# Transposing q, k and u of two batches by DMA inside SBUF instead of on TensorE

## The chip, the cores and the metric

The kernel runs on one core of one Trainium2 chip. The metric is device time in microseconds (us) of one execution. The core has five instruction streams, each of which runs its own list in order: TensorE (PE), VectorE (DVE), ScalarE (ACT), GpSimd (POOL) and SyncE (SP), which here only issues DMAs. Matrix products land in PSUM (eight banks of 2 KB per partition); everything else lives in SBUF (128 partitions).

## The reference

Two layers follow each other, for 4 batches of 768 positions. The first is a gated linear recurrence over 8 heads of width 48:

```python
for t in range(S):
    state = alpha[:, :, t, :, None] * state + np.einsum('bhd,bhe->bhde', k[:, :, t], v[:, :, t])
    y[:, :, t] = np.einsum('bhd,bhde->bhe', q[:, :, t], state)
```

Its output, with the heads side by side, is x of shape (4, 768, 384). The second layer mixes along the positions with a matrix of rank 32 and then applies a two-layer perceptron (384 to 1536 to 384):

```python
xt = x.transpose(0, 2, 1)
h = xt @ U @ V
u = x + h.transpose(0, 2, 1)
ch = np.maximum(u @ w_ch1, 0.0) @ w_ch2
return u + ch
```

## The kernel before

**Tiling.** Each batch is cut into 6 chunks of 128 positions, and the recurrence works on 2 chunks at a time: three stages per batch, `stage_gla`, twelve in all. Within a chunk the recurrence becomes matrix products. ScalarE takes the logarithm of alpha (L350, tile lt), TensorE sums it along the positions (L358, L360), and ScalarE makes exp of the sums and of their negatives (aa and ai, L368 and L369). k is multiplied by ai and q by aa (L374), which gives rk and rq, with positions on the partitions and every head padded from 48 to 64 columns. For the score product (L406) both must stand with the head dimension on the partitions. So TensorE transposes each 128x128 block of rk and of rq (L383, 8 blocks for k and 8 for q in a stage) into a PSUM bank, and ScalarE (L289) or VectorE (L291) copies the bank to SBUF as kt and qt. VectorE masks the scores (L416, tile pm), TensorE makes the update of the state (L441, L448), which VectorE scales (L451, tile st), and y from state and scores (L468, L474), which ScalarE writes to xb (L486).

**Mixing.** `stage_mix` makes the rank-32 product (L499, L506, tile utx). The first batch has a path of its own. For the other three, TensorE multiplies utx with V for each chunk (L524), VectorE adds that to xb (L525), which gives u, and TensorE transposes u in three groups of 6 blocks (L534), which ScalarE copies to uT (L542).

**Perceptron.** `mlp1` makes 24 groups of 3 products per batch (L553), each 384 columns wide, with the relu on ScalarE (L563) or VectorE (L565). `mlp2` makes 6 output chunks of 12 products (L574), adds u on VectorE (L583, tile ou) and stores (L584).

**Order.** A planner at build time (`Plan.run`) sets the order of all of it. Each operation is added with its engine, a cost in nanoseconds, what it reads and writes, and a priority (lower goes first). The planner simulates the engines with these costs and writes each engine's operations out in the order in which it started them. On the chip each engine then keeps that list strictly, whatever the real durations are. An engine whose next instruction waits does nothing else. Buffers are rotating pools, so a tile may also wait until the earlier user of its slot is done.

**Transfers.** All DMAs go through SP's one list: for each batch alpha, k, q and v, 1.18 MB each in runs of 192 bytes (48 float32 values), the six parts of the two weight matrices (768 KB each, cast to bfloat16 on GpSimd, L291), the two small matrices U and V, and 24 stores of 192 KB. A store waits in that list for VectorE's sum, and whatever stands behind it waits too.

**Fill.** Up to the first batch's mixing, the planner puts products without use (L587) into TensorE's gaps.

Of the kernel before, what the change touches and what calls it, by code (L numbers as in the profile page):

```python
# [49 lines left out]
class Op:  # L50
    __slots__ = ("eng", "cost", "fn", "prio", "deps", "bufs", "n", "end", "users", "est", "i")


class Plan:
# [11 lines left out]
    def add(self, eng, cost, fn, r=(), w=(), prio=0.0, after=(), kind=None):  # L66
# [24 lines left out]
        op.bufs = []  # L91
        for k in list(r) + list(w):
            b = k[0] if isinstance(k, tuple) else k
            if isinstance(b, Buf) and b not in op.bufs:
                op.bufs.append(b)
        for b in op.bufs:
            b.left += 1
        self.ops.append(op)
        return op

    def run(self):
# [8 lines left out]
        clock = {}  # L110
# [4 lines left out]
        while todo:  # L115
# [42 lines left out]
            if eng == "SP":  # L158
                clock[eng] = max(t + 450.0, dma)
# [29 lines left out]
def kernel(  # L189
# [50 lines left out]
    u_in = const.tile([128, NC, R], FP32, name="u_in")  # L240
    vm_in = const.tile([128, S], FP32, name="vm_in")
# [16 lines left out]
    pms = Pool(slots("pm", 4, [C, 2, HP, C], BF16))  # L258
# [3 lines left out]
    uts = Pool(slots("uT", 2, [128, NCT, S], BF16))  # L262
# [17 lines left out]
    mlps = [every, every, every, every]  # L280
# [12 lines left out]
    def load_low_rank():  # L293
        P.add("SP", 500, lambda: nc.sync.dma_start(u_in, moe_U.rearrange("(c p) r -> p c r", p=128)), w=["u_in"], prio=0.3)
        for g in range(4):
            P.add("SP", 400, lambda g=g: nc.sync.dma_start(vm_in[32 * g : 32 * g + R, :], moe_V), w=[("vm_in", g)], prio=0.3)
        P.add("POOL", 350, lambda: nc.gpsimd.tensor_copy(u_sb, u_in), r=["u_in"], w=["u"], prio=300)
        P.add("POOL", 820, lambda: nc.gpsimd.tensor_copy(vm_sb, vm_in), r=[("vm_in", g) for g in range(4)], w=["vm"], prio=300)

    def load_big():  # L300
# [6 lines left out]
        for i, (src, dst) in enumerate(parts):  # L307
# [7 lines left out]
            P.add("SP", 2000, lambda src=src, stage=stage: nc.sync.dma_start(stage(), src), w=[(t, i)], prio=0.5 if i < 3 else 0.6)  # L315
# [14 lines left out]
    def stage_gla(b, g, sprev, xb, ins):  # L330
# [59 lines left out]
        for src, dst, eng, cost in ((rk, kT, "ACT", 1015), (rq, qT, eqt, 1015 if eqt == "ACT" else 640)):  # L390
            tb = Buf(gen)
# [100 lines left out]
    def stage_mix(b, xb, uT):  # L492
# [14 lines left out]
        if b == 0:  # L507
            P.fill_end = op
            for hf in range(2):
                for j in range(NCT):  # L510
# [9 lines left out]
                    P.add(eng, 550 if eng == "DVE" else 490, lambda hf=hf, j=j, tb=tb, eng=eng: copy(eng, uT()[:, j, hf * TW : (hf + 1) * TW], tb()[:, 0, 0:TW]), r=[tb], w=[(uT, hf, j)], prio=pr)  # L520
            return utx
        for c in range(NC):
            hb = Buf(mlp)
            P.add("PE", mm(DM), lambda c=c, hb=hb: nc.tensor.matmul(hb()[:, 0, 0:DM], lhsT=vm_sb[:, c * C : (c + 1) * C], rhs=utx(), start=True, stop=True), r=[utx, "vm"], w=[hb], prio=pr + 1)  # L524
            P.add("DVE", 550, lambda c=c, hb=hb: nc.vector.tensor_tensor(xb()[:, c, :], xb()[:, c, :], hb()[:, 0, 0:DM], op=ALU.add), r=[hb, (xb, c)], w=[(xb, c)], prio=pr)  # L525
            if c % 2 == 1:
# [12 lines left out]
                def f_ev(c=c, ub2=ub2):  # L539
                    t = bf(ub2())[:, 0 : 2 * NCT * C].rearrange("p (c2 j t) -> p c2 j t", c2=2, j=NCT)  # L540
                    dst = uT()[:, :, (c - 1) * C : (c + 1) * C].rearrange("p j (c2 t) -> p c2 j t", c2=2)
                    nc.scalar.copy(dst, t)  # L542
# [3 lines left out]
    def mlp1(b, uT, h1, tt):  # L546
        for jt in range(NJ):
            hb = Buf(mlps[b])
            pr = 5000 + b * 1000 + tt * 100 + jt * 8

            def f(jt=jt, hb=hb):
                for ct in range(NCT):
                    nc.tensor.matmul(  # L553
                        hb()[:, 0, 0:TW], lhsT=w1_sb[:, ct, jt * 128 : (jt + 1) * 128],
                        rhs=uT()[:, ct, tt * TW : (tt + 1) * TW], start=(ct == 0), stop=(ct == NCT - 1),
# [3 lines left out]
            if b == 0:  # L559
                need = [(uT, tt, j) for j in range(NCT)]  # L560
            P.add("PE", mm(TW, TW, TW), f, r=need + [("w1", jt // 4)], w=[hb], prio=pr)
# [5 lines left out]
    def mlp2(b, xb, h1, c, utx):  # L567
        hb = Buf(mlps[b])
        pr = 5000 + b * 1000 + 100 + (c % 3) * 33 + (0 if c < 3 else 100)
        for g in range(3):  # L570

            def f(g=g):
                for jt in range(4 * g, 4 * g + 4):
# [4 lines left out]
                if g == 2 and utx is not None:  # L578
                    nc.tensor.matmul(hb()[:, 0, 0:DM], lhsT=vm_sb[:, c * C : (c + 1) * C], rhs=utx(), start=False, stop=True)

            P.add("PE", mm(*[DM] * (5 if g == 2 and utx is not None else 4)), f, r=([utx] if utx is not None else []) + [(h1, jt) for jt in range(4 * g, 4 * g + 4)] + [("w2", g)], w=[hb], prio=pr + g)
# [51 lines left out]
```

## Time and profile before

| | |
|---|---|
| median of 3 runs | 181.5 us (180.69 to 182.88) |
| the profiled execution | 180.38 us |
| its span, first to last instruction | 178.7 us |
| TensorE busy in the span | 166.2 us (93%) |
| VectorE, ScalarE, GpSimd busy | 94.0, 86.5, 52.7 us |
| share of TensorE in the chain that ended last | 65% |
| share of waits for DMA in that chain | 17% |

The profiled execution took 1.7 us more than its span, and 1.1 us less than the median. A matmul's busy time (326 ns for 384 columns) is the time from its start to its modelled end. Matmuls overlap, so the time that one adds to a dense row of them is read from the chain, which merges such a row: 39 of L553 took 6.34 us, 163 ns each.

### The profile page before, as it was taken

What the parts mean: (1) busy time and instruction counts of PE and PEld (TensorE: products, weight loads), DVE (VectorE), ACT (ScalarE), POOL (GpSimd) and SP (SyncE); (2) the same over time, 40 slices, a digit from 0 to 9 for tenths busy, and PEclk for the clock granted to TensorE, in tenths of its full rate; (3) what the DMA queues carried; (4) which work ended last, traced back from release to release, by engine and by line L of the source; (5) the groups of instructions that cost most, each with busy time, mean ns of one, the idle gap of its engine ahead of it and who ended that gap; (6) DMA issues with size and microseconds to landing.
All of it is one profiled execution on the core that took longest, in us unless ns stands there. A gap on an engine that the chain in (4) does not pass through costs nothing.

```text
span 178.7 us, 4275 instructions
## 1 busy us (share of the span) xinstructions
PE 166.2 (93%) x1821; PEld 107.8 (60%) x1821; DVE 94.0 (53%) x159; ACT 86.5 (48%) x142; POOL 52.7 (29%) x52
## 2 busy tenths in 40 slices
PE   5997888999999996988999999999999999999992
PEld 4775665555666754655666566755566565656560
DVE  2022991643327775458676577667485432544421
ACT  2387684645891344894783847401555310422200
POOL 4000197760469600497416567000000000000000
PEclk9999999999999999699999999999999999999999
DMA  4987999996977868899889300111101112101212
GB/s 111 262 257 221 261 287 391 370 321 191 261 224 225 254 204 246 275 259 262 257 230 252 117 15 33 48 46 44 48 0 44 48 46 88 44 0 48 85 49 88
DMA packets 32068, 29.08 MB, mean 163 GB/s; under 512 B 1584, under 2 KB 30768, under 8 KB 32048
## 3 DMA queue, kind: packets, MB, share of 16 engines
q1 hardware_dynamic: 32048, 28.81, 53.5%
q8 instruction: 14, 0.23, 0.6%
q14 instruction: 6, 0.05, 0.1%
HBM read 24.08 MB, written 4.72 MB: 161 GB/s over the span
## 4 chain that ended last, share of the span: by engine, by line
PE 65%; DMA 17%; SPq 6%; DVE 5%; ACT 3%; issue 2%; POOL 1%; DVEq 0%; ACTq 0%; POOLq 0%
PE ps L553 24%; PE ps L574 22%; DMA io<-in_alpha_dram 7%; DMA io<-in_q_dram 6%; SPq L327 4%; DMA io<-in_v_dram 4%; PE ps L474 3%; PE ps L383 3%; DVE pm L416 3%; PE ps L406 3%; SPq L584 2%; PE ps L468 2%; PE ps L441 1%; PE ps L524 1%; ACT lt L350 1%
## 5 line engine op out<-in xcount | busy, mean ns | idle before, releaser
L553 PE MATMUL ps<-uT,w_sb 128*128 128x384 bf16 x288 | 52.9, 326 | 0.0
L574 PE MATMUL ps<-w_sb,h1t 128*128 128x384 bf16 x288 | 52.4, 326 | 0.0
L563 ACT ACTIVATE h1t<-ps 128x384 bf16<-128x384 f32 x48 | 23.7, 493 | 37.7 <-PE ps L553 37.4
L574 PEld LDWEIGHTS <-h1t 128*128 128x128 bf16 x288 | 27.2, 98 | 17.1 <-issue 0.3
L553 PEld LDWEIGHTS <-w_sb 128*128 128x128 bf16 x288 | 26.9, 98 | 16.2 <-issue 0.3
L565 DVE TENSOR_SCALAR h1t<-ps 128x384 bf16<-128x384 f32 x48 | 26.7, 557 | 16.6 <-PE ps L553 14.8
L416 DVE TENSOR_TENSOR pm<-ps,maskc 128x1024 bf16<-128x1024 f32 x22 | 26.8, 1221 | 5.5 <-PE ps L406 4.9
L583 DVE TENSOR_TENSOR ou<-xb,ps 128x384 f32<-128x384 bf16 x24 | 13.3, 553 | 29.2 <-PE ps L574 20.5
L374 POOL TENSOR_TENSOR rk<-io,ai 128x768 bf16<-128x768 f32 x9 | 14.8, 1643 | 25.7 <-ACT ai L368 18.9
L289 ACT COPY kt<-ps 128x1024 bf16<-128x1024 bf16 x12 | 12.1, 1015 | 13.1 <-PE ps L383 6.1
L291 POOL CAST rv<-io 128x768 bf16<-128x768 f32 x12 | 9.6, 829 | 23.6 <-DMA io<-in_v_dram 23.6
L486 ACT CAST xb<-ps 128x768 bf16<-128x768 f32 x12 | 9.6, 798 | 13.8 <-PE ps L474 13.7
L374 POOL TENSOR_TENSOR rq<-io,aa 128x768 bf16<-128x768 f32 x9 | 14.8, 1645 | 4.1 <-DMA io<-in_q_dram 2.1
L587 PE MATMUL ps<-fill_in,ident 128*128 128x256 bf16 x87 | 13.6, 316 | 1.9 <-POOL ident masks.py:199 1.9
L350 ACT ACTIVATE lt<-io 128x768 bf16<-128x768 f32 x12 | 9.6, 841 | 9.7 <-DMA io<-in_alpha_dram 9.7
L525 DVE TENSOR_TENSOR xb<-xb,ps 128x384 bf16<-128x384 bf16 x18 | 9.5, 550 | 6.0 <-PE ps L524 5.9
L587 PEld LDWEIGHTS <-ident 128*128 128x128 bf16 x87 | 9.4, 113 | 4.1 <-POOL ident masks.py:199 1.9
L368 ACT ACTIVATE ai<-ps 128x768 bf16<-128x768 f32 x12 | 9.9, 822 | 0.3 <-PE ps L360 0.3
L369 ACT ACTIVATE aa<-ps 128x768 bf16<-128x768 f32 x12 | 10.0, 830 | 0.0
L291 POOL CAST w_sb<-io 128x1536 bf16<-128x1536 f32 x6 | 8.8, 1469 | 3.9 <-DMA io<-in_moe_w_ch_dram 3.9
L474 PE MATMUL ps<-rv,pm 128*128 128x48 bf16 x192 | 8.9, 184 | 1.1 <-DVE pm L416 1.1
L406 PE MATMUL ps<-qt,kt 48*128 48x128 bf16 x192 | 9.0, 218 | 0.5 <-ACT xb L486 0.5
(57 smaller groups left out, 157.4 us busy)
## 6 DMA issues: line engine op xcount, KB each, us to landing
io<-in_moe_w_ch_dram SPq DMA_DIRECT2D x6, 768.0 KB, 9.7
out_dram<-ou SPq DMA_DIRECT2D x24, 192.0 KB, 1.9
vm_in<-in_moe_V_dram SPq DMA_DIRECT2D x4, 96.0 KB, 2.6
u_in<-in_moe_U_dram SPq DMA_DIRECT2D x1, 96.0 KB, 6.1
io<-in_alpha_dram SPq DMA_DIRECT2D x4, 0.2 KB, 11.3
io<-in_k_dram SPq DMA_DIRECT2D x4, 0.2 KB, 10.2
io<-in_q_dram SPq DMA_DIRECT2D x4, 0.2 KB, 10.5
io<-in_v_dram SPq DMA_DIRECT2D x4, 0.2 KB, 8.9
```

The source lines that it names most:

```text
L289: nc.scalar.copy(dst, src)
L291: ENG[eng].tensor_copy(dst, src)
L374: ENG[eng].tensor_tensor(dst()[:, :, :, 0:D], ch(src), fac().rearrange("t g (h d) -> t g h d", d=D), op=ALU.mult)
L406: nc.tensor.matmul(s2[:, par, p, :], lhsT=kT()[o : o + D, i, p, :], rhs=qT()[o : o + D, i, p, :], start=(p == 0), stop=(p == HP - 1),)
L416: nc.vector.tensor_tensor(pmi().rearrange("t two hp c -> t (two hp) c"), sc().rearrange("p two (hp c) -> p (two hp) c", c=C), maskc.to_bro ...
L474: nc.tensor.matmul(y2[:, par, p, :], lhsT=pm[i]()[:, par, p, :], rhs=rv()[:, i, 2 * p + par, :], start=(i == 0 and p == 0 and last is None ...
L553: nc.tensor.matmul(hb()[:, 0, 0:TW], lhsT=w1_sb[:, ct, jt * 128 : (jt + 1) * 128], rhs=uT()[:, ct, tt * TW : (tt + 1) * TW], start=(ct == ...
L563: P.add("ACT", 500, lambda jt=jt, hb=hb: nc.scalar.activation(h1()[:, jt, :], hb()[:, 0, 0:TW], AF.Relu), r=[hb], w=[(h1, jt)], prio=100)
L565: P.add("DVE", 560, lambda jt=jt, hb=hb: nc.vector.tensor_scalar_max(h1()[:, jt, :], hb()[:, 0, 0:TW], 0.0), r=[hb], w=[(h1, jt)], prio=100)
L574: nc.tensor.matmul(hb()[:, 0, 0:DM], lhsT=h1()[:, jt, (c % 3) * C : (c % 3 + 1) * C], rhs=w2_sb[:, jt, :], start=(jt == 0), stop=(jt == NJ ...
L583: P.add("DVE", 550, lambda: nc.vector.tensor_tensor(ou(), xb()[:, c, :], hb()[:, 0, 0:DM], op=ALU.add), r=[hb, (xb, c)], w=[ou], prio=100)
L587: P.fill_fn = lambda i: nc.tensor.matmul(ps[:, i, 0:256], lhsT=ident, rhs=fill_in, start=True, stop=True)
```

## The change

For the third and fourth batch (b = 2 and 3; batches are counted from 0 in the code and below) three kinds of transpose leave TensorE, and one DMA instruction on SP does each instead, from SBUF to SBUF. In each of these batches' six stages there is one for rk to kt and one for rq to qt, 128 partitions by 1024 elements (256 KB, 8 blocks). In the mixing there are two per batch, from xb to uT, 128 by 1152 elements (288 KB, 9 blocks). With the 132 TensorE transposes their copies out of PSUM go too: 6 of L289 and 6 of L542 on ScalarE and 6 of L291 on VectorE. There are 16 transposing DMAs in all.

The same edit changes some other things. In batch 1 q is scaled on VectorE instead of GpSimd, and its transposed copy is made on ScalarE instead of VectorE. The pool of masked scores has 6 slots instead of 4. uT is laid out by chunk instead of by block of columns. U and V are staged in a slot of the load pool. The three loads of the second weight matrix get a later priority. In batch 0's mlp1 the second half comes sooner, and mlp2's last product of batch 0 (L579 before) is an operation of its own.

```diff
-        op.i = len(self.ops)
+        op.i, op.hold = len(self.ops), hold
...
             if eng == "SP":
-                clock[eng] = max(t + 450.0, dma)
+                clock[eng] = max(t + op.hold, dma)
...
-    u_in = const.tile([128, NC, R], FP32, name="u_in")
-    vm_in = const.tile([128, S], FP32, name="vm_in")
...
-    pms = Pool(slots("pm", 4, [C, 2, HP, C], BF16))
+    pms = Pool(slots("pm", 6, [C, 2, HP, C], BF16))
...
-    uts = Pool(slots("uT", 2, [128, NCT, S], BF16))
+    uts = Pool(slots("uT", 2, [128, NC, NCT, C], BF16))
...
     def load_low_rank():
-        P.add("SP", 500, lambda: nc.sync.dma_start(u_in, moe_U.rearrange("(c p) r -> p c r", p=128)), w=["u_in"], prio=0.3)
+        t = Buf(io)
+
+        def u_in():
+            return t()[:, 0 : NC // 2, :].rearrange("p a (two r) -> p (a two) r", r=R)
+
+        def vm_in():
+            return t()[:, 16:28, :].rearrange("p a w -> p (a w)")
+
+        P.add("SP", 500, lambda: nc.sync.dma_start(u_in(), moe_U.rearrange("(c p) r -> p c r", p=128)), w=[(t, 4)], prio=0.3)
...
-            P.add("SP", 2000, lambda src=src, stage=stage: nc.sync.dma_start(stage(), src), w=[(t, i)], prio=0.5 if i < 3 else 0.6)
+            P.add("SP", 2000, lambda src=src, stage=stage: nc.sync.dma_start(stage(), src), w=[(t, i)], prio=0.5 if i < 3 else 1.15)
...
         ek = "DVE" if first else "POOL"
-        eq = "DVE" if first else "POOL"
+        eq = "DVE" if b in (0, 1) else "POOL"
         ev = "POOL"
-        eqt = "ACT" if first else "DVE"
-        split = (-1, 1, 1)[g] if first else -1
+        eqt = "ACT" if b in (0, 1) else "DVE"
+        split = (-1, 1, 1)[g] if b in (0,) else -1
...
         for src, dst, eng, cost in ((rk, kT, "ACT", 1015), (rq, qT, eqt, 1015 if eqt == "ACT" else 640)):
+            if b in (2, 3):
+                P.add("SP", 1000, lambda src=src, dst=dst: nc.sync.dma_start_transpose(dst().rearrange("p g e c -> p (g e) c"), src().rearrange("t g h w -> t (g h w)")), r=[src], w=[dst], prio=pr / 1000 - 1, hold=1250.0)
+                continue
             tb = Buf(gen)
...
             P.add("DVE", 550, lambda c=c, hb=hb: nc.vector.tensor_tensor(xb()[:, c, :], xb()[:, c, :], hb()[:, 0, 0:DM], op=ALU.add), r=[hb, (xb, c)], w=[(xb, c)], prio=pr)
+            if b in (2, 3):
+                if c % 3 == 2:
+                    P.add("SP", 1100, lambda c=c: nc.sync.dma_start_transpose(uT()[:, c - 2 : c + 1].rearrange("p c j t -> p (c j) t"), xb()[:, c - 2 : c + 1, :].rearrange("p c m -> p (c m)")), r=[(xb, c - i) for i in range(3)], w=[(uT, c // 3, j) for j in range(NCT)], prio=pr / 1000 - 1, hold=1300.0)
+                continue
             if c % 2 == 1:
...
-            pr = 5000 + b * 1000 + tt * 100 + jt * 8
+            pr = 5000 + b * 1000 + tt * (100 if b else 50) + jt * (8 if b else 4)
...
-                        rhs=uT()[:, ct, tt * TW : (tt + 1) * TW], start=(ct == 0), stop=(ct == NCT - 1),
+                        rhs=uT()[:, 3 * tt : 3 * tt + 3, ct, :], start=(ct == 0), stop=(ct == NCT - 1),
...
-            if b == 0:
+            if b == 0 or b in (2, 3):
                 need = [(uT, tt, j) for j in range(NCT)]
```

The planner writes a new order from this. The first place is SP's list around the loads of batches 2 and 3; line numbers are those of each kernel's own file. Before, from the last two stores of batch 0, the loads of v of batch 2 (io_88) and of alpha, k, q and v of batch 3 stand in a row:

```order
L584 DMA out_dram<-ou_150 128x384
L584 DMA out_dram<-ou_151 128x384
L327 DMA io_88<-in_v_dram 128x48x48
L327 DMA io_89<-in_alpha_dram 128x48x48
L327 DMA io_90<-in_k_dram 128x48x48
L327 DMA io_91<-in_q_dram 128x48x48
L327 DMA io_86<-in_v_dram 128x48x48
L584 DMA out_dram<-ou_149 128x384
```

In the changed program the same stretch, from the first transposing DMA on (L398 is the transpose, L333 a load, L596 a store):

```order
L398 DMA_TRANSPOSE kt_123<-rk_98 128x8x128
L333 DMA io_86<-in_v_dram 128x48x48
L398 DMA_TRANSPOSE qt_126<-rq_93 128x8x128
L398 DMA_TRANSPOSE kt_124<-rk_99 128x8x128
L398 DMA_TRANSPOSE qt_127<-rq_94 128x8x128
L398 DMA_TRANSPOSE kt_125<-rk_96 128x8x128
L398 DMA_TRANSPOSE qt_128<-rq_95 128x8x128
L333 DMA io_88<-in_alpha_dram 128x48x48
L333 DMA io_89<-in_k_dram 128x48x48
L596 DMA out_dram<-ou_149 128x384
L333 DMA io_84<-in_q_dram 128x48x48
L333 DMA io_85<-in_v_dram 128x48x48
```

The load of batch 2's v now stands behind the first transpose, and all four loads of batch 3 stand behind six transposes. Each of these waits for a product of GpSimd (rk or rq).

The second place is the list of GpSimd after the casts of the first weight matrix (tile w_sb from 128x3x512 is the first matrix, from 128x1536 the second; rk and rq are the products of batch 1). Before:

```order
L291 CAST w_sb<-io_90 128x3x512 x2
L291 CAST w_sb<-io_91 128x3x512
L291 CAST w_sb<-io_91 128x1536
L291 CAST w_sb<-io_86 128x1536 x2
L374 TENSOR_TENSOR rk_101<-io_88,ai_118 128x16x48
L374 TENSOR_TENSOR rk_98<-io_88,ai_119 128x16x48
L374 TENSOR_TENSOR rq_95<-io_89,aa_115 128x16x48
```

And in the changed program, with L289 the cast and L380 the product:

```order
L289 CAST w_sb<-io_89 128x3x512 x2
L289 CAST w_sb<-io_84 128x3x512
L380 TENSOR_TENSOR rk_99<-io_86,ai_116 128x16x48
L289 CAST w_sb<-io_84 128x1536
L380 TENSOR_TENSOR rk_96<-io_86,ai_117 128x16x48
L289 CAST w_sb<-io_87 128x1536 x2
L380 TENSOR_TENSOR rk_97<-io_86,ai_118 128x16x48
```

The casts of the second weight matrix now come between the products for k of batch 1, and the three products for q have left the list. On SP the loads of the second matrix stand, likewise, behind those of alpha and k of batch 1.

On TensorE the list is the same up to batch 0's mlp1. In batch 2, before, the scores of the first stage stood behind 6 products of that batch's predecessor's mlp1 (L553); now they stand behind 39 of them in a row. In batch 3 now the first scores also stand behind 39 (L564 in the new file), of batch 2's mlp1, and the 16 small products of the state's update.

More of the change, by code (lines that the diff above doesn't have):

```diff
@@ L50 @@
 class Op:
-    __slots__ = ("eng", "cost", "fn", "prio", "deps", "bufs", "n", "end", "users", "est", "i")
+    __slots__ = ("eng", "cost", "fn", "prio", "deps", "bufs", "n", "end", "users", "est", "i", "hold")
 class Plan:
@@ L279 @@
     mlp0 = banks((6,), (7,), (4,), (5,))
-    mlps = [every, every, every, every]
+    mlps = [banks(*[(i,) for i in s]) for s in (range(8),) * 4]
     def bf(bank):
@@ L569, in mlp2 @@
         pr = 5000 + b * 1000 + 100 + (c % 3) * 33 + (0 if c < 3 else 100)
[L570 removed]
+        for g in range(NJ // 4):
             def f(g=g):
[L573 removed]
+                for jt in range(4 * g, 4 * (g + 1)):
                     nc.tensor.matmul(
@@ L577, in f @@
                     )
-                if g == 2 and utx is not None:
-                    nc.tensor.matmul(hb()[:, 0, 0:DM], lhsT=vm_sb[:, c * C : (c + 1) * C], rhs=utx(), start=False, stop=True)
-            P.add("PE", mm(*[DM] * (5 if g == 2 and utx is not None else 4)), f, r=([utx] if utx is not None else []) + [(h1, jt) for jt in range(4 * g, 4 * g + 4)] + [("w2", g)], w=[hb], prio=pr + g)
+            P.add("PE", mm(*[DM] * 4), f, r=[(h1, jt) for jt in range(4 * g, 4 * (g + 1))] + [("w2", g * 4 // 4)], w=[hb], prio=pr + g)
+        if utx is not None:
+            P.add("PE", mm(DM), lambda: nc.tensor.matmul(hb()[:, 0, 0:DM], lhsT=vm_sb[:, c * C : (c + 1) * C], rhs=utx(), start=False, stop=True), r=[utx], w=[hb], prio=pr + 9)
         ou = Buf(outs)
```

21 lines of the change are left out of this document (10 added, 11 removed).

## The prediction

> **What bounds the kernel now.** I read the page first, for the shares and the slices, then a table by stretch, then the chain of waits.
>
> ```profile
> span 178.7 us, 4275 instructions
> ...
> PE 166.2 (93%) x1821; PEld 107.8 (60%) x1821; DVE 94.0 (53%) x159; ACT 86.5 (48%) x142; POOL 52.7 (29%) x52
> ...
> PE   5997888999999996988999999999999999999992
> ...
> PEclk9999999999999999699999999999999999999999
> DMA  4987999996977868899889300111101112101212
> ```
>
> TensorE is busy 93% of the span, without a hole in the second half. The DMA engines are the opposite: near full until the 22nd slice (98 us), then almost idle. So an average says little, and the stretches must be read apart (PE, PEld, DVE, ACT, POOL, granted clock, DMA share, GB/s):
>
> ```profile
> 47.00:65.00 18.00, 17.83 (x227) 11.84 (x226) 10.87 (x17) 8.07 (x14) 12.08 (x9) 1.00 0.80 234
> 65.00:82.00 17.00, 14.63 (x199) 9.78 (x198) 9.41 (x16) 13.66 (x22) 7.07 (x5) 0.90 0.87 249
> 82.00:100.00 18.00, 17.20 (x271) 11.25 (x271) 12.92 (x20) 10.63 (x18) 8.25 (x7) 1.00 0.91 260
> 100.00:175.00 75.00, 75.00 (x657) 45.94 (x654) 40.22 (x70) 26.39 (x48) 8.82 (x7) 1.00 0.12 43
> ```
>
> From 100 to 175 us TensorE is busy all of the time, and from 82 to 100 it lacks 0.8 us. Only from 65 to 82 us is there a gap of 2.4 us, with a granted clock of 0.90. So what leaves TensorE in batches 2 and 3 should leave the time, unless TensorE's fixed list then waits for something. The chain of waits, in order of time, gives what each piece costs there:
>
> ```profile
> 32.59 6.40 PE ps L553 x39
> ...
> 74.64 6.65 DMA io<-in_v_dram
> ...
> 90.25 0.45 PE ps L383 x8
> ...
> 91.70 0.17 PE ps L358
> 91.94 0.18 PE ps L358
> 92.20 0.24 PE ps L441 x8
> 92.44 0.19 PE ps L448
> ...
> 95.99 0.20 PE ps L468 x8
> 96.19 0.31 PE ps L474 x8
> 96.50 0.33 PE ps L406 x8
> ...
> 100.82 0.43 PE ps L499 x6
> ...
> 109.03 0.34 PE ps L534 x6
> ...
> 151.72 6.34 PE ps L553 x39
> ```
>
> A product of 384 columns costs 6.34 / 39 = 0.163 us in the dense row, eight transposes of k or q 0.45 us, and six of u 0.34 us; a chunk's running sum with its four narrow products takes 0.25 (from 91.70 to 91.94 and on to 92.20). The time at 74.64 is the load of batch 2's v, the one place after 72 us where the chain runs through a DMA.
>
> **What leaves TensorE.** Per stage 8 transposes of rk and 8 of rq, in six stages: 12 groups of eight. In the mixing 3 groups of six per batch: 6 groups. So 12 x 0.45 + 6 x 0.34 = 5.4 + 2.0 = **7.4 us**. Of the twelve, four stand before 82 us, where TensorE is not full; if those gave nothing, 5.6 us would be left. ScalarE and VectorE lose their copies too:
>
> ```profile
> L289 ACT COPY kt<-ps 128x1024 bf16<-128x1024 bf16 x12 | 12.1, 1015 | 13.1 <-PE ps L383 6.1 <-DVE ou L583 4.1 <-issue 2.8
> ...
> L542 ACT COPY uT<-ps 128x768 bf16<-128x768 bf16 x9 | 7.2, 800 | 3.8 <-PE ps L534 3.8
> ...
> L291 DVE COPY qt<-ps 128x1024 bf16<-128x1024 bf16 x9 | 6.2, 684 | 2.5 <-PE ps L383 1.3 <-ACT uT L542 1.2
> ```
>
> That is 6 x 1.0 + 6 x 0.8 = 10.9 us of ScalarE and 6 x 0.68 = 4.1 us of VectorE, both half idle in these stretches; I count nothing for it. In batch 1 q's scaling moves between these two rows:
>
> ```profile
> L374 POOL TENSOR_TENSOR rq<-io,aa 128x768 bf16<-128x768 f32 x9 | 14.8, 1645 | 4.1 <-DMA io<-in_q_dram 2.1 <-PE ps L524 1.9
> ...
> L374 DVE TENSOR_TENSOR rq<-io,aa 128x768 bf16<-128x768 f32 x3 | 2.8, 955 | 3.3 <-DMA io<-in_q_dram 3.3
> ```
>
> GpSimd loses 3 x 1.65 us and VectorE gains 3 x (0.96 - 0.68) = 0.8 us, while ScalarE takes 3 x 1.0 us of copies. From 47 to 65 us VectorE is busy 10.9 of 18 us and ScalarE 8.1, so that hides; without the cover it would cost at most those 0.8 and 3 us. Six slots for pm and the other layouts move no bytes that anyone waits for: zero.
>
> **What one transposing DMA costs.** The trace has none. Call p the time for which one keeps SP's list or the DMA engines, whichever is longer. The nearest rows are the loads and the stores, on the same queue (start and held time of SP, then size and time to landing):
>
> ```profile
> 69.16 5.27 SPq L584 DMA_DIRECT2D out_dram<-ou  x2
> 74.64 0.70 SPq L327 DMA_DIRECT2D io<-in_v_dram  x1
> 75.80 4.12 SPq L327 DMA_DIRECT2D io<-in_alpha_dram  x1
> 80.38 4.20 SPq L327 DMA_DIRECT2D io<-in_k_dram  x1
> 85.04 4.36 SPq L327 DMA_DIRECT2D io<-in_q_dram  x1
> 89.86 4.18 SPq L327 DMA_DIRECT2D io<-in_v_dram  x1
> ...
> out_dram<-ou SPq DMA_DIRECT2D x24, 192.0 KB, 1.9
> ```
>
> Loads follow each other every 4.7 us (80.38 to 85.04). One is 6,144 runs of 192 bytes, 1.18 MB. A transpose moves 256 KB in 1,024 rows of 256 bytes: by runs 4.7 / 6 = 0.8 us, by bytes 1.0 us. If the crossing cuts it into pieces of 32 bytes, 8,192 runs, it is 6.3 us. So p lies between 0.8 and 6.3 us. I take 1.2, near the byte figure, since a run's length and its end in SBUF are close to the load's; the code's planner reckons 1.25, a number of the code that no row confirms. A store lands 1.9 us after its issue, of which 0.8 is its bytes: 1.1 us for landing.
>
> These rows are the ground for a fast transpose, and one rule speaks against it. The Trainium skill (VectorE: DVE Perf Modes, section on the three transpose paths) gives a DMA transpose of one 128x128 block 1,309 ns against 390 ns on TensorE, and advises TensorE where PSUM will do. If the eight blocks each paid that, p would be 10.5 us (an estimate from that page), and the sum would end near 265 us; no run here shows it. On its side the trace has TensorE's block at 0.45 / 8 = 0.06 us in a dense row, far below that page's 390 ns.
>
> **Where TensorE waits for the transposes.** Batch 2 begins where GpSimd makes its first product, and mlp1 of batch 1 fills TensorE:
>
> ```profile
> 38.80 1.47 POOL L291 CAST w_sb<-io 128x1536 bf16<-128x1536 f32 x1 [0.67 <-DMA io<-in_moe_w_ch_dram]
> ...
> 71.86 1.64 POOL L374 TENSOR_TENSOR rk<-io,ai 128x768 bf16<-128x768 f32 x1 [10.46 <-ACT ai L368]
> 75.43 1.64 POOL L374 TENSOR_TENSOR rq<-io,aa 128x768 bf16<-128x768 f32 x1 [1.94 <-PE ps L524]
> ...
> 78.23 0.65 PE L553 MATMUL ps<-uT,w_sb 128*128 128x384 bf16 x3
> ```
>
> rk is made at 73.5 us, so the first transpose issues at about 74.6, where v's load stood. v's load follows (4.7 us), then q's transpose, which lands at 74.6 + p + 4.7 + p + 1.1 = 80.4 + 2p: 82.8 us. TensorE starts mlp1 at 78.2 and has 39 products ahead of the scores, to 84.6. No wait up to p = 2.1. The next two pairs have 12 and 16 wide products and some groups of eight (0.2 to 0.33 us each) between them: 4.1 and 5.1 us against 2p.
>
> The tighter place is batch 3. Its loads stand behind six transposes: alpha issues at 79.3 + 6p = 86.5 us instead of 75.8 (GpSimd's last product, five of 1.65 us after 75.4, is ready at 83.7). v then issues at 100.6; before, it issued at 89.9 and GpSimd began its cast at 100.1, so now it lands at 110.8 and its cast ends at 111.6. TensorE's list first needs it for the state's update of batch 3. From 84.6 us stand ahead of that, in the changed list, 111 products of 384 columns (18.1 us), 22 groups of eight (6.0 us), four of L448, six running sums and L499 (2.7 us): 111.4 us. That is a wait of **0.2 us**, and 6 us more for each microsecond of p. For batch 3's own transposes the DMA engines are idle (share 0.12), and TensorE's 39 products with the 16 small ones give 6.9 us for the first pair; 3.9 and 4.7 us for the others. The transposes of u have 32 and more wide products (5.2 us) against 1.1p + 1.1: hidden.
>
> **The second weight matrix.** Its loads come behind alpha and k of batch 1, 8.4 to 9.4 us later. Its last part landed at 38.8 before, so now at 47.2 to 48.2, and is cast by 48.7 to 49.7. TensorE starts mlp1 of batch 0 at 32.6, has 72 products (11.7 us), two stages' sums and one group of transposes (1.5 us) and 1.7 us of other products ahead: 47.5. A wait of 1.2 to 2.2 us. The 2.4 us of gap between 65 and 82 us can take some of it, since batch 1 starts earlier: I count **1.0 us**.
>
> **Sum.** 180.4 - 7.4 + 0.2 + 1.0 = 174.2 us for a profiled execution; the median lies 1.1 above it, so **175.3 us**. What is late next is still TensorE's list, with the same end.
>
> **Rivals.**
>
> *Faster than that* (under 173): nothing is lost in front, and the gap from 65 to 82 us closes because k of batch 1 comes earlier: 180.4 - 7.4 - 2.4 = 170.6 to 173. Against it stands the second weight matrix. Chance 0.07.
>
> *It evens out.* p is about 1.95 to 2.4. Then TensorE waits 0.2 + 6 x (p - 1.2) for batch 3's v, 4.7 to 7.4 us, and the 7.4 are gone: 180 to 182.5 us. For it: nothing in the trace crosses partitions by DMA. Chance 0.09.
>
> *Slower.* p above 2.4; one mechanism, batch 3's loads queued behind six transposes on SP while TensorE's list waits. At p = 3, v costs 0.2 + 10.8 = 11.0, and batch 3's later pairs (6 us against 3.9 and 4.7) 3.4: 180.4 - 7.4 + 1.0 + 14.4 + 1.1 = 189.5 us. It decides from p = 2.2, where it equals the gain. A waiting TensorE may also run slower after it, as the 6 in the clock row, at 71 to 76 us, stands in the one stretch with gaps. Chance 0.11.
>
> *Block by block.* Eight landings in series, 8 x 1.1 + 1.0 = 9.8 us. Batch 3's v would come 52 us late, its six transposes take 59 us, and two of u and one mlp follow: about 260 us. The rows say that a 192 KB store pays its landing once, not per piece. This is the result that the skill's block price, above, would give. Chance 0.03.
>
> **How the numbers follow.** My forecast (p up to 1.95) has the remaining 0.70, from 173 to 180 us. About 1% (1.8 us) is what a measurement of this kernel can tell from no change. Faster by over 1%: 0.70 + 0.07 = 0.77. Within 1%: 0.09. Slower: 0.11 + 0.03 = 0.14. The range reaches down to 171 us, into the faster case, and up to 183.5, past the one that evens out; it leaves out the slower cases (0.14) and the lowest few hundredths.
>
> **What would show it.** TensorE's rows L383 and L534 should fall by 96 and 36. The new DMA rows on SP should be held 1 to 1.5 us each and land 2 to 3 us after issue; at 2 us or more the forecast fails. TensorE's waits before the scores of batches 2 and 3 should be under 1 us, and its wait for the cast of v (rv) near 0.2. A wait for the cast of the second weight matrix near 48 us should be 1 to 2 us. From 110 us to the end TensorE should be full. If a wait stands in front of the scores, or alpha of batch 3 issues later than 90 us, p was wrong; if the list is full and the time is not shorter, the 0.45 us per group was.

## The result

| | before | changed |
|---|---|---|
| median | 181.91 us (180.69 to 182.88) | 175.68 us (175.09 to 176.59) |
| the profiled execution | 180.38 us | 176.59 us |
| its span | 178.7 us | 174.9 us |
| TensorE busy in the span | 166.2 us | 161.0 us |

The ratio is 0.9665, with a 95% interval of 0.9585 to 0.9746. The kernel was run twice more beside later experiments, against the kernel before on the same chip: 0.9605 (0.9524 to 0.9686) and 0.957 (0.946 to 0.9681). The mean of the three is 0.961. A ratio leaves out executions more than 1.5% above the fastest of the same kernel; in the third comparison these are two of four, at 177.0 and 177.6 us. The forecast was 175.3 us.

In the changed kernel the line numbers are higher: the transposes L383 and L534 are L389 and L547 now, the scores are L415, the update of the state L450, mlp1 L564, mlp2 L586, its sum and store L595 and L596, the loads L333, and the new DMAs L398 (k and q) and L537 (u).

The page of the changed kernel (busy time of each engine, granted clock and DMA share in 40 slices):

```profile
span 174.9 us, 4027 instructions
...
PE 161.0 (92%) x1689; PEld 101.2 (58%) x1689; DVE 91.2 (52%) x153; ACT 79.3 (45%) x133; POOL 47.6 (27%) x49
...
PEclk9999996599999999999969999999999999999999
DMA  3788989979988967698898987999910128101212
```

TensorE has 132 instructions fewer, 96 of L389 and 36 of L547, as the change says. The DMA row stays near full up to the 29th slice (127 us), where it was almost idle after 98 us before. The clock row shows two dips: near 30 us, in front of everything that the change touches, and near 90 us. The table by stretch, for the same stretches as before (the columns are TensorE, weight loads, VectorE, ScalarE and GpSimd busy, granted clock, DMA share, GB/s):

```profile
47.00:65.00 18.00, 17.79 (x216) 11.39 (x214) 10.32 (x14) 11.45 (x17) 7.06 (x7) 1.00 0.85 250
65.00:82.00 17.00, 15.85 (x193) 9.51 (x188) 10.59 (x19) 10.52 (x20) 6.83 (x5) 1.00 0.76 216
82.00:100.00 18.00, 15.12 (x198) 8.78 (x195) 10.71 (x17) 5.38 (x9) 5.20 (x5) 0.91 0.90 219
100.00:175.00 75.00, 70.92 (x625) 42.06 (x623) 39.49 (x69) 22.60 (x44) 12.02 (x9) 0.99 0.49 122
```

Half of the old gap between 65 and 82 us has closed (15.85 us busy, 14.63 before). A new one has opened between 82 and 100 us: 15.12 busy, 17.20 before. What it is stands in the timeline of TensorE (start, time, line; in brackets the wait ahead of it and what ended it):

```profile
77.64 6.50 PE L564 MATMUL ps<-uT,w_sb 128*128 128x384 bf16 x39
87.02 0.62 PE L415 MATMUL ps<-qt,kt 48*128 48x128 bf16 x16 [2.88 <-DMA qt<-rq]
...
88.81 1.41 PE L586 MATMUL ps<-w_sb,h1t 128*128 128x384 bf16 x4
```

The first scores of batch 2 wait 2.88 us for q's transposed tile. And 1.8 us after that, four products of mlp2 take 1.41 us instead of the 0.82 that the four before them took: from 88.6 to 92 us the granted clock is 0.54. The timeline of SP shows what the new DMAs cost there (start, and how long SP was held):

```profile
70.82 5.51 SPq L596 DMA_DIRECT2D out_dram<-ou  x3
76.43 1.35 SPq L398 DMA_TRANSPOSE kt<-rk  x1
78.23 0.71 SPq L333 DMA_DIRECT2D io<-in_v_dram  x1
79.06 5.85 SPq L398 DMA_TRANSPOSE qt<-rq  x1
85.01 1.28 SPq L398 DMA_TRANSPOSE kt<-rk  x1
86.39 1.29 SPq L398 DMA_TRANSPOSE qt<-rq  x1
87.78 1.27 SPq L398 DMA_TRANSPOSE kt<-rk  x1
89.16 1.27 SPq L398 DMA_TRANSPOSE qt<-rq  x1
90.89 0.70 SPq L333 DMA_DIRECT2D io<-in_alpha_dram  x1
...
111.87 1.31 SPq L537 DMA_TRANSPOSE uT<-xb  x1
```

With nothing in front, a transpose of eight blocks holds SP for 1.28 us and the next follows after 1.39. The one behind v's load is held 5.85 us, until that load has gone. Landing, from the page's list of DMA issues (the last column is the median time from issue to landing, in us):

```profile
kt<-rk SPq DMA_TRANSPOSE x6, 3.4
qt<-rq SPq DMA_TRANSPOSE x6, 3.3
```

### The profile page after: what moved, and what is told of

Read it like the earlier page. It is cut to its first block, busy times and chain, and to the rows that moved or that the text cites. A ratio compares the mean times of both kernels' runs of the same rounds, so it can differ in the third digit from the quotient of the medians.

```text
span 174.9 us, 4027 instructions
## 1 busy us (share of the span) xinstructions
PE 161.0 (92%) x1689; PEld 101.2 (58%) x1689; DVE 91.2 (52%) x153; ACT 79.3 (45%) x133; POOL 47.6 (27%) x49
## 4 chain that ended last, share of the span: by engine, by line
PE 54%; DMA 22%; SPq 12%; ACT 5%; DVE 3%; issue 1%; POOL 0%; DVEq 0%
PE ps L586 23%; PE ps L564 17%; DMA io<-in_q_dram 13%; SPq L333 9%; DMA qt<-rq 4%; DMA out_dram<-ou 4%; SPq L321 3%; PE ps L415 3%; PE ps L483 3%; PE ps L389 2%; PE ps L477 2%; PE ps L450 1%; PE ps L533 1%; ACT ai L374 1%; DVE rq L380 1%; ACT uT L553 1%
## 5 line engine op out<-in xcount | busy, mean ns | idle before, releaser
L586 PE MATMUL ps<-w_sb,h1t 128*128 128x384 bf16 x288 | 54.3, 331 | 0.0
L564 PE MATMUL ps<-uT,w_sb 128*128 128x384 bf16 x288 | 51.1, 326 | 0.1
L586 PEld LDWEIGHTS <-h1t 128*128 128x128 bf16 x288 | 27.3, 99 | 17.6 <-issue 0.8
L564 PEld LDWEIGHTS <-w_sb 128*128 128x128 bf16 x288 | 27.0, 97 | 16.9 <-issue 0.2
L595 DVE TENSOR_TENSOR ou<-xb,ps 128x384 f32<-128x384 bf16 x24 | 13.2, 551 | 25.3 <-PE ps L586 20.3
L380 POOL TENSOR_TENSOR rk<-io,ai 128x768 bf16<-128x768 f32 x9 | 14.8, 1640 | 39.3 <-ACT ai L374 39.3
L289 POOL CAST rv<-io 128x768 bf16<-128x768 f32 x12 | 9.6, 825 | 24.6 <-DMA io<-in_v_dram 24.6
L534 DVE TENSOR_TENSOR xb<-xb,ps 128x384 bf16<-128x384 bf16 x18 | 9.4, 550 | 4.6 <-PE ps L533 4.5
L415 PE MATMUL ps<-qt,kt 48*128 48x128 bf16 x192 | 8.8, 218 | 2.9 <-DMA qt<-rq 2.9
L380 POOL TENSOR_TENSOR rq<-io,aa 128x768 bf16<-128x768 f32 x6 | 9.8, 1639 | 2.2 <-DMA io<-in_q_dram 2.2
L289 POOL CAST w_sb<-io 128x1536 bf16<-128x1536 f32 x6 | 8.7, 1465 | 2.7 <-DMA io<-in_moe_w_ch_dram 2.7
L483 PE MATMUL ps<-rv,pm 128*128 128x48 bf16 x192 | 9.5, 190 | 0.0
L415 PEld LDWEIGHTS <-kt 48*128 48x128 bf16 x192 | 5.4, 94 | 6.6 <-issue 6.0
```

The lines of the kernel that those rows point to most:

```text
L289: ENG[eng].tensor_copy(dst, src)
L380: ENG[eng].tensor_tensor(dst()[:, :, :, 0:D], ch(src), fac().rearrange("t g (h d) -> t g h d", d=D), op=ALU.mult)
L415: nc.tensor.matmul(s2[:, par, p, :], lhsT=kT()[o : o + D, i, p, :], rhs=qT()[o : o + D, i, p, :], start=(p == 0), stop=(p == HP - 1),)
L483: nc.tensor.matmul(y2[:, par, p, :], lhsT=pm[i]()[:, par, p, :], rhs=rv()[:, i, 2 * p + par, :], start=(i == 0 and p == 0 and last is None ...
L564: nc.tensor.matmul(hb()[:, 0, 0:TW], lhsT=w1_sb[:, ct, jt * 128 : (jt + 1) * 128], rhs=uT()[:, 3 * tt : 3 * tt + 3, ct, :], start=(ct == 0 ...
L586: nc.tensor.matmul(hb()[:, 0, 0:DM], lhsT=h1()[:, jt, (c % 3) * C : (c % 3 + 1) * C], rhs=w2_sb[:, jt, :], start=(jt == 0), stop=(jt == NJ ...
```

## The experiments

Theory A, the prediction's: the gain is the transposes that leave TensorE's full list, less what TensorE waits in batch 2. Theory B: the other edits (order of loads, q of batch 1 on VectorE, more slots) make the gain. Later theory C: up to the landing of batch 3's v, near 110 us, SP's queue and TensorE's list end nearly together, so a wait that is taken away there shows the next one. All kernels compute the whole result. The pieces below are read as differences of ratios, whose intervals reach about 1 point to each side (1.8 us); they are sizes to that precision.

**The other edits alone.** No transpose goes by DMA; all else stays.

```diff
-            if b in (2, 3):
+            if b in ():
```

(in all three places, for q and k, for u, and for what mlp1 waits for)

> All other edits of the change, and every transpose left on TensorE. Theory A (the time falls because 7.4 us of transposes leave TensorE's full list, less a wait of 2.9 us for the first q transpose of batch 2): close to before, 180 to 182 us. Theory B (the other edits and the new order of the loads make the gain, the transposes are incidental): 175.5 to 177 us, as the changed kernel.

Measured: 0.9929 (0.9891 to 0.9967), 179.12 us against 180.33. The other edits give 0.7 points, 1.3 us. The time is 0.9 us below the range expected by theory A and 2.1 above that of theory B. The page of this kernel:

```profile
span 176.6 us, 4275 instructions
...
PE 164.6 (93%) x1821; PEld 106.9 (61%) x1821; DVE 94.6 (54%) x159; ACT 89.3 (51%) x145; POOL 47.7 (27%) x49
```

Its table by stretch:

```profile
65.00:82.00 17.00, 15.85 (x218) 10.20 (x217) 11.17 (x18) 11.73 (x20) 9.92 (x8) 1.00 0.90 266
```

TensorE gets 15.85 us of work done between 65 and 82 us, 1.2 more than before, at full clock. So the half of the old gap that closed belongs to the other edits, not to the DMAs. The clock of this stretch was 0.90 before and is 1.00 here; what of the 1.2 us is order and what is clock was not separated. Theory B falls as the main cause: most of the gain is missing here.

**Only q and k, only u.** The first keeps u's transposes on TensorE, the second those of q and k.

For only q and k:

```diff
             P.add("DVE", 550, lambda c=c, hb=hb: nc.vector.tensor_tensor(xb()[:, c, :], xb()[:, c, :], hb()[:, 0, 0:DM], op=ALU.add), r=[hb, (xb, c)], w=[(xb, c)], prio=pr)
-            if b in (2, 3):
+            if b in ():
...
-            if b == 0 or b in (2, 3):
+            if b == 0 or b in ():
```

> The changed kernel with u's transposes back on TensorE (36 blocks, 6 x 0.34 = 2.0 us). Theory A: 2.0 us above the changed kernel, 177 to 178.5 us, with the wait before batch 2's first scores still there. Theory B: 175.5 to 176.5 us.

For only u:

```diff
         for src, dst, eng, cost in ((rk, kT, "ACT", 1015), (rq, qT, eqt, 1015 if eqt == "ACT" else 640)):
-            if b in (2, 3):
+            if b in ():
```

> The changed kernel with q's and k's transposes back on TensorE; only u goes by DMA. Theory A: 2.0 us below the kernel with no DMA transposes, 178 to 180 us, and no wait before the scores. Theory B: 175.5 to 177 us.

Measured: q and k 0.9711 (0.9642 to 0.978), 175.12 us; u 0.9786 (0.9728 to 0.9843), 176.14 us. From the other edits alone, q and k give 2.2 points (3.9 us, where 5.4 leave TensorE) and u 1.4 (2.6 us, where 2.0 leave it). In the profile the first shows a wait of 1.5 us before batch 2's first scores and the second none. What is given back, 1.5 us, goes with q and k as far as the precision tells. In absolute time both missed theory A's ranges from below, by 1.9 us each, and u alone lies inside that of theory B; what speaks against theory B is the step from the other edits alone to these two.

**Only batch 3, only batch 2.**

The same three places, for batch 3 alone (for batch 2 alone it is `(2,)`):

```diff
-            if b in (2, 3):
+            if b in (3,):
```

> DMA transposes in batch 3 alone, batch 2 back on TensorE. Theory A: half of the 7.4 us is gained (3.7) but batch 2's wait of 2.9 us and up to 1.1 us of slower clock behind it are not paid: 176 to 178 us, within 1.5 us of the changed kernel; the DMA transposes of batch 2 are worth almost nothing. A rival (each batch's transposes bring the same half of the gain): halfway between e1 and the changed kernel, 3 us above the latter.

> DMA transposes in batch 2 alone, batch 3 back on TensorE. Theory A: 3.7 us leave TensorE, and the first q transpose of batch 2, queued behind v's 4.7 us load, takes back 2.9 us and up to 1.1 us of slower clock: 0 to 1 us below the kernel with no DMA transposes, that is 1 to 2.5 us below before, and 3 to 4.5 us above the changed kernel. The rival (each batch's transposes bring half): 2.5 us above the changed kernel, and no wait of more than 1 us before batch 2's scores.

Measured: batch 3 alone 0.9725 (0.9636 to 0.9814), 174.82 us; batch 2 alone 0.9824 (0.9726 to 0.9922), 178.7 us. The four executions of batch 2 alone took 177.3, 177.4, 180.0 and 180.7 us, and its ratio rests on the first two. From 0.9929, batch 3 gives 2.0 points (3.7 us; 3.7 leave TensorE) and batch 2 gives 1.05 (1.9 us; also 3.7 leave). Their sum is 5.6 us, and all together gave 5.7 (0.9929 less the mean of 0.961). So, to the precision of these ratios, the two add up, batch 3 pays in full, and what is given back, some 1.8 us, is in batch 2. By the median of all four executions batch 2 would give 0.4 us only. Batch 3 alone came below its expected range; by the ratios it is 2.1 us above the changed kernel, between theory A (up to 1.5) and the rival (3). Batch 2 alone is 3.9 us above the changed kernel that ran beside it, as theory A said. The profiled executions agree on batch 3: a span of 176.6 us for the other edits alone and 172.9 us here. The table for batch 3 alone:

```profile
100.00:128.00 28.00, 28.00 (x336) 16.67 (x333) 18.50 (x31) 12.19 (x21) 5.13 (x5) 1.00 0.43 87
```

TensorE has no hole there, and no wait over 0.4 us stands after 77 us. ScalarE and VectorE lose their copies in the same step, and no run separates that; but before, TensorE was busy all of the time from 100 to 175 us, so no wait stood there that fewer copies could have taken away. The profiled execution of batch 2 alone is the one of 180.7 us; it waits 4.5 us before the first scores.

**The changed kernel again, beside the next two.**

> The changed kernel again, on the same chip as the next three, as their yardstick: 0.9665 of before, so 174 to 176 us. Nothing is told apart by it.

Measured: 0.9605, 173.37 us, 0.6 below the range expected; its span is 171.3 us. Its page:

```profile
PE 157.5 (92%) x1689; PEld 99.2 (58%) x1689; DVE 90.9 (53%) x153; ACT 78.8 (46%) x133; POOL 47.7 (28%) x49
```

Its timeline of TensorE:

```profile
84.27 0.62 PE L415 MATMUL ps<-qt,kt 48*128 48x128 bf16 x16 [1.15 <-DMA qt<-rq]
```

Its timeline of VectorE:

```profile
111.03 0.55 DVE L595 TENSOR_TENSOR ou<-xb,ps 128x384 f32<-128x384 bf16 x1 [2.50 <-DMA out_dram<-ou]
```

Its mean clock is 0.990 and that of the other edits alone is 0.987, so these two pages can be set beside each other. TensorE's busy time falls from 164.6 to 157.5 us, by 7.1, where the prediction had 7.4. The rest of the span, in which it is not busy, grows from 176.6 - 164.6 = 12.0 to 171.3 - 157.5 = 13.8 us, by 1.8. The net is 5.3 us, of a like size to the 5.7 from the ratios.

The wait is 1.15 us here and 2.88 in the first profile. The order of instructions is the same. In the first profile q's load held SP 6.74 us and here 4.29, the first transpose issued at 76.43 and here at 73.59, while mlp1 of batch 1 began at 77.64 and 76.63: SP had slipped by 2.8 us and TensorE by 1.0. Over five profiles the wait goes with that load: held 4.29 us with a wait of 1.15, 4.68 with 1.5 (q and k alone), 6.74 with 2.9, 6.85 with 3.6 (the changed kernel's third profile), 6.86 with 4.5 (batch 2 alone). From 66 to 70 us the DMA engines moved 202 GB/s in the first profile and 239 in the second. Why, stays open.

**q's first transpose ahead of most of v's load.** Batch 2's v is loaded in six DMAs of one chunk each, chunks 0 and 1 before q's first transpose and chunks 2 to 5 behind it.

```diff
+        order.insert(tr[1] + 1, (order[tr[1]][0], rest))
...
+            if (b, n) == (2, 3):
+                P.parts = [lambda part=part: part(0, G), lambda part=part: part(G, NC)]
+                f = P.parts[0]
```

> The changed kernel's lists, with one difference on SP: of batch 2's v only the two chunks that the first stage needs are loaded ahead of q's first transpose (1.6 us of transfer instead of 4.7), and the other four behind it. If the wait of 2.9 us comes from that load being ahead in the queue, q's transpose lands 3 us sooner, near 83.7 us, and the wait before the scores goes; GpSimd's cast of v, behind six products until 85.6, then leaves up to 1.1 us. So 1.5 to 3 us below the changed kernel. If the wait is the transpose's own landing time, nothing changes.

Measured: 0.9639 (0.9542 to 0.9736), 174.47 us: no gain over the changed kernel that ran beside it (0.9605), where 1.5 to 3 us had been expected from the wait of 2.9. The kernel beside it waited only 1.15 us, so that much was all that could be gained from this wait, and it is inside the interval. Its timeline of TensorE:

```profile
87.32 0.40 PE L430 MATMUL ps<-qt,kt 48*128 48x128 bf16 x8 [0.81 <-DMA qt<-rq]
```

And of VectorE:

```profile
111.33 1.07 DVE L610 TENSOR_TENSOR ou<-xb,ps 128x384 f32<-128x384 bf16 x2 [3.90 <-DMA out_dram<-ou]
```

The wait before the first scores is gone. The second pair's scores (L430 is L415 here) wait 0.81 us in its place, and further on VectorE's sum ou waits 3.90 us for its slot, 2.50 in the kernel above. The list of waits has 1.3 us of TensorE (L465) behind that sum. SP's list gets through no sooner: alpha of batch 3 issues at 87.89 us (88.01 above), v at 100.45 in both. And TensorE ends the 16 products of this state's update (L465 here, L450 above) at 112.8 us in both. This is where theory C comes from. The store that frees ou's slot stands behind v's load in SP's list; VectorE's sum waits for the slot, and TensorE for the sum.

**Batch 2's q and k of stages 0 and 1 back on TensorE.**

```diff
-            if b in (2, 3):
+            if b in (2, 3) and (b == 3 or g > 1):
```

> The changed kernel with the first two stages of batch 2 back on TensorE (4 groups, 1.8 us more there); its third stage, u of both batches and all of batch 3 stay on DMA. Theory A: the wait of 2.9 us goes, 1.8 us come back: 0 to 2 us below the changed kernel. The rival that transposes simply pay by the piece: 1.8 us above it.

Measured: 0.965 (0.9564 to 0.9735), 174.12 us: neither the gain of up to 2 us nor the loss of 1.8 us stands outside the interval. No wait of TensorE for a transposing DMA is left, and 1.8 us of transposes are back on TensorE (4 groups of 0.45): the two may cancel.

**All of batch 2's q and k back on TensorE**, with the changed kernel once more.

In the place for q and k alone, so that u stays by DMA in both batches:

```diff
-            if b in (2, 3):
+            if b in (3,):
```

> The changed kernel again, as the yardstick of this chip: 173 to 175.5 us. Its wait before batch 2's first scores was 2.9 us in one execution and 1.15 in another, so it should lie between 1 and 3 us again.

> q and k of batch 2 back on TensorE (2.7 us more there), all of batch 3 and u of both batches by DMA. Theory C, formed from the last runs (until batch 3's v has landed near 112 us TensorE's list and the queue of loads and transposes on SP end nearly together, so taking one wait away exposes the next): the queue gets 8.3 us shorter and TensorE's list 2.7 longer, TensorE alone decides: within 1 us of the changed kernel. If TensorE's waits in batch 2 and 3 were all paid one after the other: 1 to 2 us below it. If TensorE's list alone counted: 2.7 us above.

Measured: 0.9591 (0.9517 to 0.9665), 174.36 us, and for the changed kernel 0.957. They are the same within the intervals, as theory C said; but a gain of 1 to 2 us, which waits paid one after the other would bring, lies inside the intervals too, so this run does not decide for theory C. No TensorE wait after 77 us is above 0.44 us. So batch 2's six transposing DMAs of q and k are worth nothing that can be measured, though they take 2.7 us (6 x 0.45) off TensorE. What batch 2 gains (1.9 us above) would then be u's share, which is 1.0 us of transposes; the rest is inside the precision. The profile of the changed kernel beside it, of an execution of 176.97 us, has a wait of 3.6 us before the first scores, more than the 1 to 3 expected, and the median of that kernel's four executions, 175.86 us, is above the range expected.

**The price of one transposing DMA.** Each transpose of q or k is cut in two DMAs of four blocks, or in eight of one block. Bytes and blocks stay the same.

For halves:

```diff
-                P.add("SP", 1000, lambda src=src, dst=dst: nc.sync.dma_start_transpose(dst().rearrange("p g e c -> p (g e) c"), src().rearrange("t g h w -> t (g h w)")), r=[src], w=[dst], prio=pr / 1000 - 1, hold=1250.0)
+                P.add("SP", 1000, lambda src=src, dst=dst: [nc.sync.dma_start_transpose(dst()[:, i], src()[:, i].rearrange("t h w -> t (h w)")) for i in range(G)], r=[src], w=[dst], prio=pr / 1000 - 1, hold=1250.0)
```

> Each transpose of q or k issued as two DMAs of 4 blocks, same order of everything else; only the price per tile changes. SP holds a transpose of 8 blocks 1.28 us and one of 9 blocks 1.31, which puts 1.04 us on the instruction and 0.03 on a block. If so, a half costs 1.16 + 0.11 us to the next issue, p = 2.5 instead of 1.39: batch 3's loads come 6 x 1.15 = 6.9 us later and its later pairs wait another 1.6, so 7 to 9 us above the changed kernel, 181 to 183 us. If the price follows the bytes, p stays 1.4 and the time stays within 1 us of the changed kernel. If the queue of loads and transposes on SP isn't what TensorE waits for, the time stays too, whatever p is.

For blocks the list runs over the pairs of heads too, `src()[:, i, 2 * p : 2 * p + 2]` for p in `range(HP)`.

> The same with eight DMAs of one 128x128 block each. From 1.04 us per instruction: 1.07 + 0.11 us per block, p = 9.4, and the walk of the rival called block by block gives 250 to 260 us. The Trainium skill's 1,309 ns for one block (VectorE: DVE Perf Modes, the three transpose paths) would make p 10.5 and the time 260 to 270 us. If single blocks are cheap, 0.2 us each, about 177 us.

Measured: halves 1.0175 (1.0092 to 1.0258), 184.94 us; blocks 277.25 us in one run. SP's timeline for halves:

```profile
86.35 2.52 SPq L398 DMA_TRANSPOSE kt<-rk  x2
88.97 2.52 SPq L398 DMA_TRANSPOSE qt<-rq  x2
...
97.94 0.74 SPq L333 DMA_DIRECT2D io<-in_alpha_dram  x1
```

The list of DMA issues on its page:

```profile
kt<-rk SPq DMA_TRANSPOSE x12, 2.5
```

SP's timeline for blocks:

```profile
101.53 10.10 SPq L398 DMA_TRANSPOSE kt<-rk  x8
111.73 10.10 SPq L398 DMA_TRANSPOSE qt<-rq  x8
```

Its list of waits (total, times, longest):

```profile
PE ps L415 <- DMA qt<-rq: 76.7, 41, 9.7
```

The clock row of its page:

```profile
PEclk9999999999997557557557799955755755899999
```

From one instruction to the next SP takes (111.73 - 101.53) / 8 = 1.28 us with one block, (88.97 - 86.35) / 2 = 1.31 with four and 1.39 with eight; the nine of u hold it 1.31 us where eight hold it 1.28. On SP the price is that of an instruction. The DMA engines show how far that goes. Their share (the number before the last) with eight blocks per instruction in the changed kernel's first profile, then with halves, then with single blocks:

```profile
85.00:90.90 5.90, 3.88 (x51) 2.47 (x52) 2.98 (x4) 0.00 (x0) 2.36 (x3) 0.83 1.00 192
86.50:97.00 10.50, 9.75 (x126) 5.33 (x121) 6.33 (x9) 1.29 (x2) 1.58 (x3) 0.68 0.49 98
102.00:111.00 9.00, 5.58 (x55) 3.09 (x55) 2.40 (x4) 0.80 (x1) 0.00 (x0) 0.69 0.13 26
```

That is 1.00 x 1.39 / 8 = 0.17 us of all DMA engines for a block, and 0.16 to 0.17 in the other two. With eight blocks the DMA engines are full as well as SP, so the price by instruction holds up to there; beyond, by these figures, the blocks would set it (an estimate; no run has more than nine). Landing grows with the blocks: 2.3 us for one, 2.4 to 2.5 for four, 3.3 to 3.4 for eight. The Trainium skill (VectorE: DVE Perf Modes, section on the three transpose paths) gives 1,309 ns for a 128x128 block by DMA; that is near what one instruction costs here, and it does not multiply with the blocks in it.

In the kernel of halves p is 2.6 us (86.35 to 88.97), where 2.5 had been expected, and it is slower by 1.75 points: the rival of batch 3's loads behind six transposes is real and has its turning point below that (the prediction put it at 2.2). The wait that these loads cause is the one for alpha, below; no wait for the cast of batch 3's v, the prediction's own, shows. Alpha of batch 3 issues at 97.94 us, 7.0 later than in the changed kernel's first profile. Against the 0.961 of the changed kernel 5.6 points, 10.2 us, are lost, more than the 7 to 9 expected. The list of waits has 5.8 us in five waits before scores, and one of 2.2 us behind ScalarE's logarithm of alpha. The granted clock is 0.50 from 88.1 to 91.5 us, behind the first two of these waits.

The kernel of blocks came out above all figures expected. TensorE waits 76.7 us for q's tiles, and between the waits the granted clock falls (0.61 from 90 to 160 us), which the forecast of that run had not in it.

## Why the prediction was right, and where not

**What leaves TensorE: 7.4 us.** Right. Busy time fell by 7.1 us at nearly the same clock, and batch 3 alone gave 3.7 us (to within 1.8), as its share of the count.

**The other edits: counted at nothing.** Too low. They gave 1.3 us, and the table shows 1.2 us of it between 65 and 82 us. GpSimd's relief was counted as hidden. Which of these edits gives the 1.3 us was not separated.

**p = 1.2 us.** Right in size: held 1.28, one per 1.39. With 0.8 to 6.3 as bounds, the row of bytes was the nearest one, and nothing near 6.3 showed. At eight blocks the DMA engines are full, so the bytes do count. But an instruction has a price of its own, 1.28 us even for one block, which was not in the prediction; that the two nearly meet at eight blocks is luck.

**Landing p + 1.1 = 2.3 us.** Too short by 1.0: it is 3.3 to 3.4. The 1.1 came from a store, and a transpose of eight blocks takes longer after its issue.

**No wait before batch 2's first scores.** This step failed, with 2.9 us in the first profile and 1.15 in the second. The prediction had the tile landed at 82.8 us; it came at 87.0. Of these 4.2 us, 1.8 are SP, which was still held by stores of batch 0 until 76.3 us where the prediction has the first issue at 74.6; 0.6 are the time from there to v's load (1.8, 1.2 counted); 0.9 are that load and q's transpose (78.23 to 85.01, 5.9 counted); and 0.9 is the landing. The margin of 1.8 us (82.8 against 84.6) was less than two such errors. The step took the old start of v's load for the first transpose's place in the list, as if the list ahead of it could not slip against TensorE.

**Batch 3's v: a wait of 0.2 us.** Near in size, but by another path. No wait for the cast of batch 3's v shows. Alpha issued at 90.9 us (88.0 in the second profile) instead of 86.5; the first is later than the 90 us which the prediction had named as a sign that p was wrong. Of these 4.4 us p has 1.1 (six times 0.19) and the late start 1.8; the rest is v's load and pauses in SP's list. TensorE's list was itself late by the wait before, so v came in time, and the one wait at this place is 0.4 us for the sum ou, whose slot waits for a store behind v's load. The prediction had not followed the stores. From there to the end of its list, at 171.3 us, TensorE is full, as forecast.

**The second weight matrix: 1.0 us.** Not paid in the first profile, where no wait for that cast shows and where the clock of 0.66 from 26 to 36 us had made TensorE 2 us late; 0.9 us in the changed kernel's third profile, and 0.8 us in the kernel with batch 2's stages 0 and 1 back on TensorE.

**Sum.** Forecast -7.4 + 0.2 + 1.0 = -6.2 us; the medians give -6.2, the two later comparisons -7.1 and -7.8 (0.0395 and 0.043 of about 181). That the first agrees to a tenth is luck among terms that cancel: the waits in batch 2 that were not counted (some 1.8 us by the ratios), against 1.3 us from the other edits and a wait for the second weight matrix that was smaller. The mechanism, the sign and the main term were right.

**The rivals.** "Slower" is what the kernel of halves shows with p = 2.6, through the wait for alpha and those before the scores. "Block by block" is what the kernel of blocks shows, 277 us for 260, but by eight issues in series, 10.2 us, and not by eight landings; the change had not its form, as one instruction takes eight blocks. "It evens out" did not come, since p stayed below 1.95.

**What stays open.** Why q's load is held longer in some executions, and with it the wait in batch 2 is 1.15, 2.9, 3.6 or 4.5 us; whether theory C holds; and whether the versions with batch 2's q and k wholly or partly on TensorE are better by a few tenths of a microsecond than the changed kernel, which is inside the intervals. None of the versions beat it beyond them.

## What to carry to other kernels

Where one engine is full without a hole, work taken off it is worth its duration in the dense row of that stretch: here about all of 3.7 us in the batch that had idle DMA engines, and half of it or less in the batch in which SP's queue was full too. A DMA transpose should be given enough blocks that the DMA engines are full, here eight, since each instruction up to there costs SP nearly the same. Ask of each new issue in a shared list what stands ahead of it, with its slips, and what stands behind it: loads, and also stores that free buffers.

## What the runs showed of the hardware

**A transposing DMA of up to eight blocks is priced by the instruction.** One follows another on SP after 1.28 us with one block, 1.31 with four and 1.39 with eight, while the landing grows from 2.3 to 3.4 us. At eight blocks the share of the DMA engines is 1.00, at 192 GB/s.

**The clock falls after a wait of some length.** The table by stretch of the changed kernel, first profile:

```profile
88.60:92.00 3.40, 3.40 (x32) 1.76 (x32) 1.91 (x4) 0.00 (x0) 0.00 (x0) 0.54 0.90 172
```

And of the second:

```profile
86.00:89.00 3.00, 3.00 (x58) 1.96 (x52) 2.52 (x5) 0.64 (x1) 0.00 (x0) 1.00 0.93 179
```

After the wait of 2.88 us the granted clock is 0.54 for 3.4 us, which costs 3.4 x 0.46 = 1.6 us more; after the wait of 1.15 us it stays at 1.00. Other profiles agree: after waits of 2.5 us (halves), 3.6 (the changed kernel's third profile) and 4.5 (batch 2 alone) the clock is 0.50 to 0.52 over 3.0 to 3.5 us, and after 1.5 us (q and k alone) it is 1.00. In the kernel with v in six DMAs, two waits of 1.3 and 0.5 us, from 110.7 to 113.2 us, are followed by 0.50 from 115 to 117 us. Where the turn lies was not measured. The prediction had named this only for the rival that is slower. Of the difference of the two spans, 3.6 us, 1.0 stands already at the start of mlp1 (77.64 and 76.63), 1.7 is the longer wait and 0.9 comes after it, so not all of the 1.6 us was paid in the end. The clock also dips near 30 us in some executions and not in others, in front of the transposes by DMA and with TensorE busy. The first profile's row:

```profile
26.00:36.00 10.00, 9.50 (x122) 6.31 (x122) 3.69 (x8) 4.92 (x8) 6.36 (x6) 0.66 0.92 314
```

In the second profile the clock of this stretch is 0.83, and before it was 1.00; what sets it was not tried.
